# Turning an operand through memory: four quadrant stores and one load, in place of one store and four loads

## The chip, the cores and the metric

The kernel runs on one core of one Trainium2 chip. The metric is device time in microseconds (us) of one execution. Five engines have a queue each: TensorE (PE, with its weight loads shown as PEld), VectorE (DVE), ScalarE (ACT), GpSimd (POOL) and SyncE (SP), which here only issues DMAs. Every DMA of this kernel stands in SP's queue, and SP works it off in order: when the DMA at its head has to wait, all that stand behind it wait too.

## The reference

Two layers, each of a linear attention block and a mixture-of-experts block (PEER, one expert per head), on 2048 rows of 576 numbers in float32:

```python
x = A_x
x = x + _A_ref(_layernorm(x, axis=-1), A_wqkv, A_wo)
x = x + _B_ref(_layernorm(x, axis=-1), B_w_q, B_k1, B_k2, B_u, B_v)
x = x + _A_ref(_layernorm(x, axis=-1), A_wqkv, A_wo)
x = x + _B_ref(_layernorm(x, axis=-1), B_w_q, B_k1, B_k2, B_u, B_v)
```

`_A_ref` multiplies by `wqkv`, takes a positive map `phi` of q and k, sums `k^T v` over all rows for 32 heads of 18, divides `q (k^T v)` by `q sum(k)`, and multiplies by `wo`. `_B_ref` scores 8 + 8 keys per head, takes the best of each, looks up one row of `u` and one of `v` (64 experts), and adds `gelu(x . u) v` over the heads.

## The kernel before

The 2048 rows are 16 tiles of 128 rows (partitions); `l` is the layer, `t` the tile. The front of a layer makes q, k and v of each tile and sums the state of the attention (`front_T`, `front_k`, `front_v`, `front_q`, `front_state`). The back of a layer divides, multiplies by `wo`, adds the residual and normalizes (`back_scale`, `back_oT`, `back_out`), scores and selects the experts (`exp_y`, `exp_scores`, `exp_select`, `exp_gelu`) and adds their output (`exp_out`). A layer's back and the next layer's front overlap: in the stretch from 290 to 480 us each step works on three tiles, the o of tile t, the b of tile t-1 and the f of layer 1 of tile t-3.

A matmul needs its operand with the contracted dimension on the partitions, so each tile is transposed three times per layer: `f` (input of q, k, v), `o` (attention output, ahead of `wo`) and `b` (input of the scores). `turned` chooses one of two ways by the table `SQUARES`. In `transposed`, TensorE does five transposes of 128 x 128. In `squares`, TensorE does nothing: VectorE transposes all 32 x 32 squares of the tile (line 229), and what is left, the exchange of whole squares between partition quadrants, goes through memory in `moved`: a store of r to a tile `y_d` in memory, and loads of it into g. Then ScalarE rounds g to the high part thi, and VectorE subtracts to get the low part tlo (`split`, lines 117 and 118). 42 turns go this way: 23 of f (twelve of layer 0, eleven of layer 1), 10 of o (layer 0, tiles 6 to 15) and 9 of b (layer 0, tiles 5 to 13). In the profile their tiles are rf, y_df, gf, thif, tlof, and the same with o and b.

The order of TensorE, ScalarE, VectorE and GpSimd is written out by hand (the strings given to `play`) and pinned by `in_order`. SP is not pinned: a scheduler places the DMAs in SP's queue by when it reckons them due. The DMAs share eight semaphores in rotation; an SP row waits for the DMA eight places ahead of it, if nothing earlier in the queue has waited for that already. `g` lies in one of two buffers taken in turn (tags uhi and ulo), and r and the normalized y share three buffers (tag y), so a buffer is written again only when the store that reads it has landed.

Other DMAs that stand beside the turns in SP's queue: `pq` (the stored phi(q) of a tile, line 441), `x` (residual input, 436), `x_d` (its result, 617), `hl_d` (the turned f kept for a later pass, 333 and 334), `fold` (weights of layer 0's front, 631).

## Time and profile before

| what | us |
|---|---|
| median of 3 runs | 719.97 |
| lowest and highest run | 719.19, 720.18 |
| the profiled execution, its time | 720.89 |
| its span in the profile | 719.1 |
| busy: TensorE / VectorE / ScalarE / GpSimd | 698.8 / 474.0 / 320.9 / 202.7 |

The granted clock of TensorE is 0.997 over the span. DMA engines are busy 46.7% of the span on average, 0.76 in the stretch 340.7 to 350.8. A row of a timeline reads: start in us, length in us, engine, line, operation, tile written <- tiles read, count, and in brackets the idle time of the engine ahead of it with what ended that. SPq rows are issues: their length is the time SP takes to hand the DMA over, and the transfer lands later.

### The profile page before, as it was taken

How to read it: one execution, taken by the hardware profiler on the slowest of the kernel's cores; microseconds unless marked ns; L12 is line 12 of the kernel's file. 1: busy time of each engine (PE TensorE's matmuls, PEld its weight loads, DVE VectorE, ACT ScalarE, POOL GpSimd, SP SyncE). 2: the span in 40 equal slices, each digit the busy share in tenths (PEclk: the TensorE clock that was granted, in tenths of full speed). 3: DMA queues.
4: the chain of work that ended last, by engine and by line, in shares of the span. 5: the costliest groups of instructions: out<-in, count | busy, mean ns of one | idle time of the engine just before them, and what ended most of it. 6: DMA issues, size and time to landing. Idle time of an engine off the chain costs nothing. (4 is left out here: it accounts for less than half of the span.)

```text
span 719.1 us, 14715 instructions
## 1 busy us (share of the span) xinstructions
PE 698.8 (97%) x5464; PEld 649.9 (90%) x5464; DVE 474.0 (66%) x1031; ACT 320.9 (45%) x658; POOL 202.7 (28%) x543
## 2 busy tenths in 40 slices
PE   8999999999999999999999999999999999999995
PEld 6999989999998999899898989899899999899984
DVE  5533343435437877687787878552647798988996
ACT  4522422342224456455555554644543534444443
POOL 2211000111004533344343433210323244433431
PEclk9999999999999999999999999999999999999998
DMA  8847777774312322476767665423632324111101
GB/s 252 274 159 249 262 237 260 253 216 137 112 33 67 100 103 102 147 232 199 238 219 234 205 198 172 138 61 121 170 106 83 112 71 134 51 67 51 51 17 66
DMA packets 82711, 107.17 MB, mean 149 GB/s; under 512 B 8976, under 2 KB 47376, under 8 KB 82640
## 3 DMA queue, kind: packets, MB, share of 16 engines
q1 hardware_dynamic: 82640, 106.24, 46.7%
q8 instruction: 43, 0.70, 0.4%
q14 instruction: 28, 0.23, 0.1%
HBM read 68.88 MB, written 37.32 MB: 148 GB/s over the span
## 5 line engine op out<-in xcount | busy, mean ns | idle before, releaser
L483 PE MATMUL ppo<-ohi,thio 126*128 126x252 f32 (+1 forms) x320 | 50.6, 300 | 3.9 <-ACT thio L117 3.9
L483 PEld LDWEIGHTS ppo<-ohi,thio 126*128 126x128 f32 (+1 forms) x320 | 44.9, 189 | 5.8 <-ACT thio L117 4.9
L188 ACT ACTIVATE junk<-x,mb 128x576 bf16<-128x576 f32 x32 | 24.8, 775 | 49.0 <-POOL mb L187 43.0
L205 ACT ACTIVATE yb<-x,rsb 128x640 f32<-128x640 f32 x32 | 29.5, 921 | 35.7 <-POOL rsb L195 35.7
L258 PE MATMUL ppk<-whi,thif 128*128 128x252 f32 (+1 forms) x300 | 45.2, 297 | 0.1
L258 PE MATMUL ppv<-whi,thif 128*128 128x252 f32 (+1 forms) x300 | 44.7, 295 | 0.1
L179 POOL TENSOR_SCALAR rsf<-mvf 128x1 f32<-128x1 f32 x16 | 3.4, 211 | 146.9 <-DVE mvf L176 146.8
L453 POOL TENSOR_TENSOR o<-pq,zb 128x576 f32<-128x576 f32 x19 | 27.3, 1439 | 60.9 <-ACT zb L399 57.4
L258 PE MATMUL ppv<-whi,tlof 128*128 128x252 f32 (+1 forms) x300 | 43.9, 293 | 0.0
L258 PE MATMUL ppk<-whi,tlof 128*128 128x252 f32 (+1 forms) x300 | 43.9, 293 | 0.0
L258 PEld LDWEIGHTS ppk<-whi,thif 128*128 128x128 f32 x300 | 40.9, 188 | 3.1 <-issue 2.9
L258 PEld LDWEIGHTS ppv<-whi,thif 128*128 128x128 f32 x300 | 41.3, 188 | 1.1 <-issue 0.4
L258 PEld LDWEIGHTS ppk<-whi,tlof 128*128 128x128 f32 x300 | 41.2, 188 | 0.0
L258 PEld LDWEIGHTS ppv<-whi,tlof 128*128 128x128 f32 x300 | 41.2, 188 | 0.0
L483 PE MATMUL ppo<-olo,thio 126*128 126x252 f32 (+1 forms) x256 | 39.6, 293 | 0.0
L258 PE MATMUL ppq<-whi 128*128 128x252 f32 (+1 forms) x260 | 39.5, 299 | 0.0
L483 PE MATMUL ppo<-ohi,tloo 126*128 126x252 f32 (+1 forms) x256 | 39.5, 293 | 0.0
L277 DVE TENSOR_SCALAR ek<-ek 128x576 f32<-128x576 f32 x16 | 7.4, 460 | 46.2 <-ACT ek L276 46.2
L258 PEld LDWEIGHTS ppq<-whi 128*128 128x128 f32 x260 | 36.0, 189 | 0.6 <-DVE eq L287 0.3
L483 PEld LDWEIGHTS ppo<-olo,thio 126*128 126x128 f32 x256 | 36.2, 188 | 0.0
L258 PE MATMUL ppk<-wlo,thif 128*128 128x252 f32 x240 | 36.1, 293 | 0.0
L258 PE MATMUL ppv<-wlo,thif 128*128 128x252 f32 x240 | 36.1, 293 | 0.0
(205 smaller groups left out, 1781.5 us busy)
## 6 DMA issues: line engine op xcount, KB each, us to landing
fold<-in_wq_t SPq DMA_DIRECT2D x64, 288.0 KB, 4.2
whi<-hl_d SPq DMA_DIRECT2D x26, 320.0 KB, 4.4
y_df<-rf SPq DMA_DIRECT2D x23, 320.0 KB, 3.0
gf<-y_df SPq DMA_DIRECT2D x92, 80.0 KB, 2.1
pq_d<-eq SPq DMA_DIRECT2D x19, 288.0 KB, 2.2
pq<-pq_d SPq DMA_DIRECT2D x19, 288.0 KB
xf<-in_x SPq DMA_DIRECT2D x16, 288.0 KB, 2.7
x<-in_x SPq DMA_DIRECT2D x16, 288.0 KB, 2.7
```

What stands on the lines that cost most here:

```text
L179: nc.gpsimd.tensor_scalar(rs[:, 0:1], mv[:, 1:2], EPS_LN, 1.0, op0=ALU.add, op1=ALU.mult)
L188: nc.scalar.activation(junk, xt, AF.Square, bias=m[:, 0:1], accum_out=m[:, 1:2])
L205: nc.scalar.activation(y, x2, AF.Identity, scale=rs[:, 0:1], bias=rs[:, 1:2])
L258: nc.tensor.matmul(o[:, at:at + c1 - c0], tt[a == "lo"][:, b, :], wb[:, cols + c0:cols + c1], start=(i == 0), stop=(i == len(todo) - 1))
L277: nc.vector.tensor_scalar(e, e, 1.0, EPS, op0=ALU.min, op1=ALU.add)
L453: nc.gpsimd.tensor_tensor(o[:, :D], pq, zb, op=ALU.mult)
L483: nc.tensor.matmul(p[:, at:at + c1 - c0], hl[a][:r, b], w[:r, c0:c1], start=(i == 0), stop=(i == len(todo) - 1))
```

## The change

`moved` lays the tile in memory out differently. Before, a row of `y_d` is a row of r, written by one store of all 128 partitions; each of four loads then fills one partition quadrant of g from pieces of 160 numbers (640 bytes) of all rows. After, a row of `y_d` is a row of g: four stores, one for each partition quadrant of r, write pieces of 640 bytes to all rows, and one load brings all 128 partitions of g as whole rows of 2560 bytes. What g holds is the same, and so are the bytes moved and the number of DMAs (five).

```diff
-        d = dr.tile([P, NB * P], F32, name=f"y_d{n}")
-        nc.sync.dma_start(d, r)
+        d = dr.tile([P, 4, NB * 32], F32, name=f"y_d{n}")
+        for q in range(4):
+            nc.sync.dma_start(d.rearrange("(j i) q x -> q i j x", j=4)[q], r[32 * q:32 * q + 32].rearrange("i (j x) -> i j x", j=4))
         yield
...
-        for j in range(4):
-            nc.sync.dma_start(g[32 * j:32 * j + 32], d.rearrange("(q i) (j x) -> j i q x", q=4, j=4)[j])
+        nc.sync.dma_start(g, d)
         return g
```

The order of instructions on TensorE, VectorE, ScalarE and GpSimd is the same before and after. SP's is not, since the scheduler places the new DMAs. In the names below the numbers are layer and tile (y_do0_9 is the o of layer 0, tile 9), the last number a buffer's.

SP's queue around the o turn of tile 9 (from about 340.7 us), before:

```order
L231 DMA y_do0_9_4473<-ro0_9_4471 128x640
L333 DMA hl_d5_93<-thif1_5_4469 128x640
L334 DMA hl_d5_93<-tlof1_5_4470 128x640
L237 DMA go0_9_4607<-y_do0_9_4473 32x4x160
L617 DMA x_d6_142<-x20_6_4489 128x576
L237 DMA go0_9_4607<-y_do0_9_4473 32x4x160
L231 DMA y_db0_8_4595<-rb0_8_4593 128x640
L237 DMA go0_9_4607<-y_do0_9_4473 32x4x160 x2
L231 DMA y_df1_6_4620<-rf1_6_4618 128x640
L237 DMA gb0_8_4622<-y_db0_8_4595 32x4x160 x4
L237 DMA gf1_6_4644<-y_df1_6_4620 32x4x160 x4
L231 DMA y_do0_10_4665<-ro0_10_4663 128x640
```

The same place of SP's queue after:

```order
L232 DMA y_do0_9_4473<-ro0_9_4471 32x4x160 x4
L617 DMA x_d6_142<-x20_6_4492 128x576
L333 DMA hl_d5_93<-thif1_5_4469 128x640
L334 DMA hl_d5_93<-tlof1_5_4470 128x640
L232 DMA y_db0_8_4598<-rb0_8_4596 32x4x160 x4
L237 DMA go0_9_4613<-y_do0_9_4473 128x640
L232 DMA y_df1_6_4623<-rf1_6_4621 32x4x160 x4
L237 DMA gb0_8_4628<-y_db0_8_4598 128x640
L441 DMA pq0_12_4894<-pq_d0_12_116 128x576
L237 DMA gf1_6_4647<-y_df1_6_4623 128x640
L232 DMA y_do0_10_4665<-ro0_10_4663 32x4x160 x4
```

All of go now stands behind all of y_db, where half of it stood ahead, and the load of pq for tile 12 has moved from behind y_do of tile 10 to the place ahead of gf. The o turns of tiles 7, 11 and 13 look alike, except that tile 13 is the last of them.

SP's queue at that last one (from about 411 us), before:

```order
L231 DMA y_db0_12_5579<-rb0_12_5577 128x640
L237 DMA go0_13_5591<-y_do0_13_5457 32x4x160 x2
L231 DMA y_df1_10_5604<-rf1_10_5602 128x640
L237 DMA gb0_12_5606<-y_db0_12_5579 32x4x160 x4
L237 DMA gf1_10_5628<-y_df1_10_5604 32x4x160 x4
L231 DMA y_do0_14_5649<-ro0_14_5647 128x640
```

and after:

```order
L232 DMA y_db0_12_5582<-rb0_12_5580 32x4x160 x4
L237 DMA go0_13_5597<-y_do0_13_5457 128x640
L232 DMA y_df1_10_5607<-rf1_10_5605 32x4x160 x4
L237 DMA gb0_12_5612<-y_db0_12_5582 128x640
L232 DMA y_do0_14_5649<-ro0_14_5647 32x4x160
L237 DMA gf1_10_5631<-y_df1_10_5607 128x640
L232 DMA y_do0_14_5649<-ro0_14_5647 32x4x160 x3
```

Here the first piece of the store y_do of tile 14 stands ahead of the load gf.

SP's queue at the first o turn (tile 6, from about 293.4 us), before:

```order
L231 DMA y_do0_6_3737<-ro0_6_3735 128x640
L231 DMA y_db0_5_3778<-rb0_5_3776 128x640
L237 DMA go0_6_3759<-y_do0_6_3737 32x4x160 x4
L617 DMA x_d3_139<-x20_3_3782 128x576
L237 DMA gb0_5_3804<-y_db0_5_3778 32x4x160 x4
L231 DMA y_df1_3_3891<-rf1_3_3889 128x640
```

and after:

```order
L232 DMA y_do0_6_3737<-ro0_6_3735 32x4x160 x4
L232 DMA y_db0_5_3778<-rb0_5_3776 32x4x160 x2
L237 DMA go0_6_3762<-y_do0_6_3737 128x640
L232 DMA y_db0_5_3778<-rb0_5_3776 32x4x160 x2
L617 DMA x_d3_139<-x20_3_3785 128x576
L232 DMA y_df1_3_3891<-rf1_3_3889 32x4x160
L237 DMA gb0_5_3807<-y_db0_5_3778 128x640
```

Half of y_db now stands behind go, and the load gb behind the first piece of the store y_df.

## The prediction

> **What bounds the kernel now.** First the page's busy times, then the list of what TensorE waits for, then the timeline of each place in that list.

> ```profile
> PE 698.8 (97%) x5464; PEld 649.9 (90%) x5464; DVE 474.0 (66%) x1031; ACT 320.9 (45%) x658; POOL 202.7 (28%) x543
> ```

> ```profile
> PE ppo L483 <- ACT thio L117: 3.9, 4, 1.4
> ```

> TensorE is busy for 698.8 of 719.1 us, and its instructions stand in the same order before and after the change. So the change can move the end only through the time TensorE waits. The first view gives the ceiling: 20.3 us of idle time in the whole run. The second says what part of it hangs on a turned operand: four waits of 3.9 us together, all of the output product (ppo) for the rounded operand thio, which ScalarE makes from the tile go. No other row of that list names a tile that passes through memory. The timeline shows where they are, and two starts that have little room:

> ```profile
> 302.58 1.59 PE L483 MATMUL ppo<-ohi,thio 126*128 126x252 f32 x10 [1.40 <-ACT thio L117]
> 318.89 1.56 PE L483 MATMUL ppo<-ohi,thio 126*128 126x252 f32 x10
> 351.57 1.59 PE L483 MATMUL ppo<-ohi,thio 126*128 126x252 f32 x10 [0.83 <-ACT thio L117]
> 384.33 1.59 PE L483 MATMUL ppo<-ohi,thio 126*128 126x252 f32 x10 [0.89 <-ACT thio L117]
> 417.05 1.59 PE L483 MATMUL ppo<-ohi,thio 126*128 126x252 f32 x10 [0.83 <-ACT thio L117]
> ```

> These are the o turns of tiles 6, 7, 9, 11 and 13. ScalarE's rows say what it waited for there:

> ```profile
> 301.80 0.73 ACT L117 ACTIVATE thio<-go 128x640 fp32r<-128x640 f32 x1
> ...
> 317.88 0.74 ACT L117 ACTIVATE thio<-go 128x640 fp32r<-128x640 f32 x1 [1.01 <-DMA go<-y_do]
> ...
> 350.78 0.74 ACT L117 ACTIVATE thio<-go 128x640 fp32r<-128x640 f32 x1 [2.38 <-DMA go<-y_do]
> ...
> 383.55 0.74 ACT L117 ACTIVATE thio<-go 128x640 fp32r<-128x640 f32 x1 [2.44 <-DMA go<-y_do]
> ...
> 416.26 0.74 ACT L117 ACTIVATE thio<-go 128x640 fp32r<-128x640 f32 x1 [2.38 <-DMA go<-y_do]
> ```

> For tile 6 the row has no idle time ahead of it (no bracket): ScalarE comes to thio from other work, so the 1.40 us there is not the memory's. For the odd tiles it sits idle until go lands, and TensorE waits behind it (for tile 7 it starts 0.27 us after thio is done at 318.62). So the landing of go in the odd tiles of this stage decides.

> **What the odd tiles' queue does.** SP's rows for tile 9, and the y_db store of the three others:

> ```profile
> 344.24 0.32 SPq L237 DMA_DIRECT2D go<-y_do  x1
> ...
> 345.69 0.34 SPq L231 DMA_DIRECT2D y_db<-rb  x1
> 346.08 2.00 SPq L237 DMA_DIRECT2D go<-y_do  x2
> ...
> 352.40 1.73 SPq L237 DMA_DIRECT2D gf<-y_df  x4
> ...
> 355.19 0.55 SPq L441 DMA_DIRECT2D pq<-pq_d  x1
> ```

> ```profile
> 314.16 0.61 SPq L231 DMA_DIRECT2D y_db<-rb  x1
> ...
> 378.56 0.41 SPq L231 DMA_DIRECT2D y_db<-rb  x1
> ...
> 411.17 0.37 SPq L231 DMA_DIRECT2D y_db<-rb  x1
> ```

> Two loads of go are issued early (344.24 is the first, when the store y_do has landed), but the last two of the four stand behind the store y_db of the next turn, which waits for VectorE's transpose of rb. From the issue of y_db to the start of thio it takes 3.72, 5.09, 4.99 and 5.09 us (317.88 - 314.16, 350.78 - 345.69, 383.55 - 378.56, 416.26 - 411.17). The order after the change puts all four pieces of y_db, and then the one load of go, at this place. The gate (rb) stays; what follows it changes.

> **The change, priced.** Per turn one store of 320 KB and four loads of 80 KB become four stores of 80 KB and one load of 320 KB: five issues either way, 210 for the 42 turns, the same bytes. Four issues in a row take 1.73 us (the gf row), 0.43 each, so a fifth starts some 1.8 us after the first. A landing is priced from these rows (KB each, median us from issue to landing):

> ```profile
> y_df<-rf SPq DMA_DIRECT2D x23, 320.0 KB, 3.0
> ...
> x<-in_x SPq DMA_DIRECT2D x16, 288.0 KB, 2.7
> ...
> x<-x_d SPq DMA_DIRECT2D x16, 288.0 KB, 3.3
> ...
> go<-y_do SPq DMA_DIRECT2D x40, 80.0 KB, 3.9
> ```

> No 320 KB load in one piece stands in the trace in this stage. 2.7 (a load of an input) is the low end, 3.9 (go itself, in the crowd of this stage) the high end. I take 3.3, since that load reads back what a store wrote, in one piece, as the new one does.

> Odd tiles, go. From the issue of y_db to thio: 1.8 + 3.3 + 0.1 = 5.2 us. Against the four numbers above this is +1.48, +0.11, +0.21 and +0.11; tile 7 has 0.27 of room, so +1.2. Sum +1.6 us. With 2.7 it is +0.6 - 0.5 - 0.4 - 0.5 = -0.8; with 3.9 it is +1.8 + 0.7 + 0.8 + 0.7 = +4.0.

> [...] The trace has both: 2.7 for 288 KB of an input, 3.3 for the same bytes written shortly before; no run here shows which the new load is like.

> Last odd tile (13), gf. For the last f of this pattern the new order puts the load of gf behind the first piece of the y_do of tile 14, which waits for VectorE's ro:

> ```profile
> 420.24 0.34 SPq L231 DMA_DIRECT2D y_do<-ro  x1
> ```

> ```profile
> 421.28 0.74 ACT L117 ACTIVATE thif<-gf 128x640 fp32r<-128x640 f32 x1 [1.98 <-DMA gf<-y_df]
> 422.61 0.78 ACT L188 ACTIVATE junk<-x,mb 128x576 bf16<-128x576 f32 x1 [0.59 <-POOL mb L187]
> ...
> 431.50 0.73 ACT L117 ACTIVATE thio<-go 128x640 fp32r<-128x640 f32 x1
> ```

> ```profile
> 432.86 1.50 PE L483 MATMUL ppo<-ohi,thio 126*128 126x252 f32 x10
> ```

> gf goes out at 420.24 + 0.4 = 420.64. The queue is empty but for one 80 KB store, so 2.7 us: thif starts at 423.4 and ends at 424.2 instead of 422.0. The squares behind it (junk) start at 424.2 instead of 422.61, 1.6 us later, and the layernorms that hang on them carry that to thio: 433.1, done at 433.8, where TensorE wants it at 432.86. So +1.0 us; +1.6 with 3.3; 0 if the chain in between has slack that I take for dependent work.

> Other odd tiles, gf. There the new order puts the load of pq ahead of gf, and pq waits for VectorE to finish reading its buffer:

> ```profile
> 352.67 0.82 DVE L461 TENSOR_TENSOR o<-pq,r 128x576 f32<-128x576 f32 x1
> ```

> ```profile
> 355.96 0.74 ACT L117 ACTIVATE thif<-gf 128x640 fp32r<-128x640 f32 x1 [1.31 <-DMA gf<-y_df]
> 357.13 0.78 ACT L188 ACTIVATE junk<-x,mb 128x576 bf16<-128x576 f32 x1 [0.43 <-POOL mb L187]
> ...
> 366.02 0.73 ACT L117 ACTIVATE thio<-go 128x640 fp32r<-128x640 f32 x1
> ```

> ```profile
> 367.38 1.50 PE L483 MATMUL ppo<-ohi,thio 126*128 126x252 f32 x10
> ```

> pq goes out at 353.5, gf at 353.9, and lands at 356.6 (2.7) to 357.2 (3.3): thif is 0.7 to 1.3 us late. junk had 0.43 of idle time ahead of it, so 0.3 to 0.9 goes on to thio, which has 0.63 of room (366.75 to 367.38). I take 0. That cover is the thinnest: beyond a landing of 3.3, three tiles lose up to 0.6 each, 1.8 us in all.

> First pair, gb of tile 5. In the new order the load of gb waits behind the first piece of y_df, for VectorE's rf:

> ```profile
> 302.40 0.34 SPq L231 DMA_DIRECT2D y_df<-rf  x1
> ```

> ```profile
> 306.39 1.40 PE L525 MATMUL kva<-shi,thib 128*128 128x512 f32 x5
> ```

> It goes out at 302.8 and lands at 305.5, thib is done at 306.3, and TensorE wants it at 306.39: 0 us, with 0.6 at a landing of 3.3. For tile 6 itself thio is held by ScalarE's own work, 0.

> The twelve f turns of layer 0, ahead of 200 us, have loads that lie long before their use:

> ```profile
> 95.20 1.75 SPq L237 DMA_DIRECT2D gf<-y_df  x4
> ```

> ```profile
> 104.26 0.73 ACT L117 ACTIVATE thif<-gf 128x640 fp32r<-128x640 f32 x1
> ```

> Loads issued until 96.95 are used at 104.26: several us of room, 0. VectorE and ScalarE wait for one DMA instead of four ahead of each split, and for four instead of one before they write a buffer that a store still reads: 0, both beside TensorE's work. No queue but SP's changes its order.

> Sum: +1.6 + 1.0 = +2.6 us. The profiled execution took 720.89 us with a span of 719.1, so it becomes 723.5 and 721.7. The median of the runs shown, 719.97, is 0.9 below the profiled one, and becomes 722.6.

> **Rivals.** *No change.* Landings go by 2.7: -0.8 + 1.0 = +0.2, 720.2 us. For it: the input loads. [...] Against it: four stores of 80 KB, just ahead of the load in the same queue, must drain first.

> *Faster.* The load of go lands as early as 2.1 to 2.2 us after its issue, because nothing is in its way once y_do, x_d and hl_d have gone out earlier. Then tiles 9, 11 and 13 lose nearly all their 0.83, 0.89 and 0.83 us, tile 7 costs nothing, and if gf of tile 13 is also covered the time is 719.97 - 2.5 = 717.5. It decides from a landing of about 2.4 us downward. Against it: no single load of this size in the rows is so quick.

> *Much slower.* Writing pieces of 640 bytes to memory may cost more than reading them. The rows that bound it, whole y_db rows written and then g loads alone in flight (DMA share and GB/s at the end):

> ```profile
> 297.75:298.25 0.50, 0.50 (x6) 0.50 (x5) 0.43 (x3) 0.38 (x1) 0.09 (x1) 1.00 0.98 379
> ...
> 96.60:98.00 1.40, 1.40 (x13) 1.40 (x12) 1.30 (x3) 0.00 (x0) 0.00 (x0) 1.00 0.79 224
> ```

> Rows of 2560 bytes are written at 379 GB/s; pieces of 640 are read at 224. I took 224 for writing them too, which the spacing of the issues hides. At half of it, 320 KB take 2.9 us instead of 1.5, go is 1.4 later in four tiles and the cover of the other odd tiles is gone: +5.6 + 1.8 on the forecast, 730 us.

> **Chances and range.** "Same" is within 0.2% (1.44 us), about what a measurement of this kernel can tell from no change. My forecast (721.4 to 725) 0.50, much slower 0.10, no change 0.27, faster 0.13. So slower 0.60, same 0.27, faster 0.13. The range takes the low ends (-0.8 and 0: 719.2) and the high ends (4.0 + 1.6 + 1.8 + 0.6 = 8.0: 728.0).

> **What would show it.** Right: TensorE's waits for thio longer than 0.9 us in tiles 11 and 13 and a new one of about 1 us in tile 7; a gap before the ppo that now starts at 432.86; thif of tile 10 near 423.4 in TensorE's unshifted time; one load of go landing 3.3 us after its issue. Wrong: waits for thio that shrink, a load that lands within 2.7 us, or stores of 80 KB whose landing passes 4 us, which would pull gb and gf after them.

## The result, and the profile after

The changed kernel takes 729.64 us (median of 4 runs, 728.96 to 730.56), the kernel before beside it 720.08 us (4 runs). The ratio is 1.0130, 95% interval 1.0116 to 1.0144: 9.4 us slower, where 2.6 us were forecast and 728.0 was the upper end of the range. The profiled execution has a span of 728.0 us against 719.1.

The busy times and TensorE's wait for thio, from the page and the list of waits:

```profile
PE 702.9 (97%) x5464; PEld 652.8 (90%) x5464; DVE 474.6 (65%) x1031; ACT 320.9 (44%) x658; POOL 202.6 (28%) x543
```

```profile
PE ppo L483 <- ACT thio L117: 7.3, 6, 1.8
```

The waits for thio have grown from 3.9 to 7.3 us. That is 3.4 of the 8.9 us in the span. TensorE's busy time has also grown, by 4.1 us, with the same instructions. TensorE's timeline at the o turns (tiles 6, 7, 9, 10, 11, 13 and 14) shows where:

```profile
303.40 1.59 PE L483 MATMUL ppo<-ohi,thio 126*128 126x252 f32 x10 [1.40 <-ACT thio L117]
...
321.70 1.59 PE L483 MATMUL ppo<-ohi,thio 126*128 126x252 f32 x10 [0.95 <-ACT thio L117]
...
355.15 1.58 PE L483 MATMUL ppo<-ohi,thio 126*128 126x252 f32 x10 [1.30 <-ACT thio L117]
...
371.30 1.59 PE L483 MATMUL ppo<-ohi,thio 126*128 126x252 f32 x10 [0.19 <-ACT thio L117]
...
389.07 1.82 PE L483 MATMUL ppo<-ohi,thio 126*128 126x252 f32 x10 [1.62 <-ACT thio L117]
...
424.49 2.79 PE L483 MATMUL ppo<-ohi,thio 126*128 126x252 f32 x10 [1.80 <-ACT thio L117]
...
441.83 1.50 PE L483 MATMUL ppo<-ohi,thio 126*128 126x252 f32 x10
```

Against the same rows of the kernel before (302.58, 318.89, 351.57, 367.38, 384.33, 417.05, 432.86) TensorE's lag is 0.82, 2.81, 3.58, 3.92, 4.74, 7.44 and 8.97 us. So 0.8 us is lost before the o turns begin, and then more with every pair of tiles. After tile 14 the lag stays. From tile 11 to tile 13 it grows by 2.70, though the wait at 13 is only 0.97 longer than before (1.80 - 0.83). From 13 to 14 it grows by 1.53 without any wait. In both places the ten matmuls take longer (1.82 and 2.79 us instead of 1.59). A table by stretches says why. Each row has the stretch and its length, the busy time of TensorE, its weight loads, VectorE, ScalarE and GpSimd with their counts, the granted clock, the DMA share and GB/s:

```profile
386.86:390.26 3.40, 1.78 (x22) 1.54 (x19) 1.34 (x4) 1.98 (x4) 0.17 (x1) 1.00 0.79 242
390.26:393.67 3.41, 3.41 (x16) 3.41 (x16) 2.22 (x3) 1.11 (x2) 0.43 (x3) 0.50 0.46 132
393.67:397.08 3.41, 3.41 (x19) 2.91 (x18) 2.33 (x4) 1.61 (x4) 0.70 (x1) 1.00 0.48 152
420.98:424.39 3.41, 1.61 (x26) 1.15 (x24) 1.15 (x4) 0.69 (x2) 0.20 (x1) 1.00 0.74 198
424.39:427.80 3.41, 3.31 (x14) 3.31 (x15) 2.90 (x5) 2.43 (x5) 0.60 (x3) 0.50 0.28 93
```

Behind each of the two longest waits TensorE runs at half clock for 3.41 us, which delays it by up to 1.7 us each (half of 3.41). Nothing in the kernel before's profile showed this: there the granted clock is at 0.50 only from 714.7 us to the end at 719.1.

The turns' other loads are late too. ScalarE's and SP's rows around tile 11:

```profile
388.28 0.74 ACT L117 ACTIVATE thio<-go 128x640 fp32r<-128x640 f32 x1 [3.14 <-DMA go<-y_do]
...
395.41 0.74 ACT L117 ACTIVATE thif<-gf 128x640 fp32r<-128x640 f32 x1 [4.04 <-DMA gf<-y_df]
```

```profile
382.44 2.55 SPq L232 DMA_DIRECT2D y_db<-rb  x4
385.03 0.43 SPq L237 DMA_DIRECT2D go<-y_do  x1
385.56 1.91 SPq L232 DMA_DIRECT2D y_df<-rf  x4
387.58 0.37 SPq L237 DMA_DIRECT2D gb<-y_db  x1
391.07 0.34 SPq L441 DMA_DIRECT2D pq<-pq_d  x1
391.62 0.32 SPq L237 DMA_DIRECT2D gf<-y_df  x1
```

Here, in tile 11, the four y_db issues take 2.55 us instead of the 1.8 I had assumed. In tiles 7, 9 and 13 they do take 1.8, but there the one issue of go takes 0.45, 0.93 and 1.21 us. In tile 11 the load of go takes from 385.03 to 388.28. gf goes out only behind pq, 4.1 us after the last store of y_df, and ScalarE idles 4.04 us for it. The new loads' landing, from the list of DMA issues:

```profile
gf<-y_df SPq DMA_DIRECT2D x23, 320.0 KB, 4.2
...
go<-y_do SPq DMA_DIRECT2D x10, 320.0 KB, 3.6
...
gb<-y_db SPq DMA_DIRECT2D x9, 320.0 KB, 3.0
```

### The profile page after: what moved, and what is told of

The parts are those of the page before. It is cut to its first block, busy times and chain, and to the rows that moved or that the text cites. A ratio compares the mean times of both kernels' runs of the same rounds, so it can differ in the third digit from the quotient of the medians.

```text
span 728.0 us, 14652 instructions
## 1 busy us (share of the span) xinstructions
PE 702.9 (97%) x5464; PEld 652.8 (90%) x5464; DVE 474.6 (65%) x1031; ACT 320.9 (44%) x658; POOL 202.6 (28%) x543
## 5 line engine op out<-in xcount | busy, mean ns | idle before, releaser
L483 PE MATMUL ppo<-ohi,thio 126*128 126x252 f32 (+1 forms) x320 | 52.2, 307 | 7.3 <-ACT thio L117 7.3
L483 PEld LDWEIGHTS ppo<-ohi,thio 126*128 126x128 f32 (+1 forms) x320 | 45.9, 193 | 9.8 <-ACT thio L117 8.9
L188 ACT ACTIVATE junk<-x,mb 128x576 bf16<-128x576 f32 x32 | 24.8, 774 | 46.9 <-POOL mb L187 40.9
L483 PE MATMUL ppo<-olo,thio 126*128 126x252 f32 (+1 forms) x256 | 40.8, 300 | 0.0
L483 PE MATMUL ppo<-ohi,tloo 126*128 126x252 f32 (+1 forms) x256 | 40.0, 295 | 0.0
L483 PEld LDWEIGHTS ppo<-olo,thio 126*128 126x128 f32 x256 | 37.6, 195 | 0.0
L118 DVE TENSOR_TENSOR tlof<-gf,thif 128x640 fp32r<-128x640 f32 x23 | 18.9, 822 | 27.4 <-ACT thif L117 27.3
L483 PEld LDWEIGHTS ppo<-ohi,tloo 126*128 126x128 f32 x256 | 36.7, 191 | 0.0
## 6 DMA issues: line engine op xcount, KB each, us to landing
fold<-in_wq_t SPq DMA_DIRECT2D x64, 288.0 KB, 4.2
pq_d<-eq SPq DMA_DIRECT2D x19, 288.0 KB, 2.1
pq<-pq_d SPq DMA_DIRECT2D x19, 288.0 KB
xf<-in_x SPq DMA_DIRECT2D x16, 288.0 KB, 2.7
x<-in_x SPq DMA_DIRECT2D x16, 288.0 KB, 2.9
```

Source lines behind the costliest of these rows:

```text
L118: eng.tensor_tensor(lo, src, hi.bitcast(F32), op=ALU.subtract)
L188: nc.scalar.activation(junk, xt, AF.Square, bias=m[:, 0:1], accum_out=m[:, 1:2])
L483: nc.tensor.matmul(p[:, at:at + c1 - c0], hl[a][:r, b], w[:r, c0:c1], start=(i == 0), stop=(i == len(todo) - 1))
```

## The experiments

Three theories were open at the start. A: what costs is the place in SP's queue, since go, gb and gf stand behind more issues. B: writing in pieces of 640 bytes is slow. C: four stores and one load are slower as such, turn by turn. Two came later: D, which is A with the four stores of y_db as what the rest is built on, and E, transfers of instructions that meet those stores. Each ratio below is to the kernel before run beside it, with its 95% interval.

**Go ahead of the y_db stores, in the changed kernel.** In the string that sets the order of the loop, the o turn's load moves ahead of the b turn's transpose:

```diff
-... v1.-2 st1.-3 bT0.1 sel0.0 gel0.0 oT0.2 v1.-2 num0.3 ...
+... v1.-2 st1.-3 oT0.2 bT0.1 sel0.0 gel0.0 v1.-2 num0.3 ...
```

> The new form, with one piece of the written-out order moved: in the odd tiles the load of go is asked for ahead of the transpose of rb, so in SP's queue it stands ahead of the four y_db stores instead of behind them. Theory A (place in the queue): the 5.7 us that TensorE waits for thio in tiles 7, 9, 11 and 13 (0.95, 1.30, 1.62, 1.80) go, and with them the two stretches of half clock (3.1 us): 729.6 - 8.8 = 720.8 us, between 719 and 723. In exchange gf of the odd tiles stands behind the first piece of the next y_do; tile 13 has that already and pays nothing. Theory B (writing in pieces of 640 bytes is slow, wherever the load stands): go, gb and gf land late as before, no more than the wait behind y_db itself is saved, and the time stays above 726 us.

Measured: 725.74 us, ratio 1.0054 (1.0033 to 1.0074). The waits for thio in tiles 7, 11 and 13 are gone, tile 9 keeps 0.72, and no half clock comes (1.00 from 388 to 395 and from 422 to 429 us). But the time falls by little more than half of what was expected, since the next operands are late in their turn: the products of tiles 8 and 10 now wait 0.44 and 0.42 us for thio, and the scores of tile 11 wait for thib. TensorE's rows of tile 11:

```profile
387.20 1.59 PE L483 MATMUL ppo<-ohi,thio 126*128 126x252 f32 x10
...
392.34 1.43 PE L525 MATMUL kva<-shi,thib 128*128 128x512 f32 x5 [1.20 <-ACT thib L117]
```

So the place of go is one part, and gb behind the stores is another.

**Whole rows in place of pieces.**

```diff
-            nc.sync.dma_start(d.rearrange("(j i) q x -> q i j x", j=4)[q], r[32 * q:32 * q + 32].rearrange("i (j x) -> i j x", j=4))
+            nc.sync.dma_start(d.rearrange("p q x -> p (q x)")[32 * q:32 * q + 32], r[32 * q:32 * q + 32])
```

> The new form with the same number, size and order of DMAs, but each of the four stores writes 32 whole rows of 2560 bytes in place of 128 pieces of 640 bytes. The exchange of squares between the partition quadrants is thereby left out, so the operands are other numbers; no instruction's size changes. Theory A (place in the queue): the same waits for thio in tiles 7, 9, 11 and 13 (each within 0.3 us), half clock at the same two places, 729.6 us within 1.5. Theory B (the pieces): stores land at least 0.5 us sooner, the four waits shrink by 0.5 us or more each, the half clock goes with them, 721 to 725 us.

Measured: 731.25 us, ratio 1.0133 (1.0108 to 1.0157), the same as the whole change; TensorE's waits for thio, in the list of waits:

```profile
PE ppo L483 <- ACT thio L117: 7.3, 7, 1.6
```

Theory B falls: in this kernel the size of the pieces costs nothing that shows (1.0133 against 1.0130). Two parts of theory A's expectation failed. The wait of tile 13 is 1.15 us instead of 1.80, and the two stretches of half clock did not come in the profiled execution of this kernel (1.00 from 388 to 395 and from 422 to 429 us). Its span is 727.0 us all the same.

**Filling the idle time.** Eight matmuls of constants ahead of the output product of tiles 11 and 13, in the changed kernel:

```diff
-        todo = sorted(out_passes(), key=lambda x: x[1]) if t == 0 else out_passes()
+        todo = sorted(out_passes(), key=lambda x: x[1]) if t == 0 else out_passes(); [nc.tensor.matmul(p[:, :252], ohi[:126, 0, :P], ohi[:126, 0, :252], start=True, stop=True) for _ in range(8 if l == 0 and t in (11, 13) else 0)]
```

> The new form, with eight extra matmuls of constants ahead of the output product of tiles 11 and 13. They lie in the time in which TensorE waits for thio there, take about 1.2 us of the 1.6 and 1.8, and are overwritten by the product. Theory A (the long idle time itself halves the clock afterwards): TensorE idles less than 0.7 us at once in these two places, the granted clock stays 1.00 there, and 3.1 us go: 726.5 us. Rival (the halved clock has another cause, or belongs to that run alone): the two stretches at half clock stay, or others come, and the time is 729.6 us within 0.7.

Measured: 729.98 us, ratio 1.0115 (1.0094 to 1.0136). That is some 1 us below the whole change's 1.0130, and the intervals overlap. TensorE's row and the stretch behind it:

```profile
387.50 1.18 PE L480 MATMUL ppo<-ohi 126*128 126x252 f32 x8
389.68 1.59 PE L483 MATMUL ppo<-ohi,thio 126*128 126x252 f32 x10 [1.01 <-ACT thio L117]
```

```profile
390.26:393.67 3.41, 3.41 (x27) 3.39 (x26) 2.81 (x6) 1.76 (x3) 0.60 (x3) 1.00 0.35 93
```

The clock stays at 1.00, as theory A says, but the 3.1 us do not come back. At full clock TensorE is earlier at the next operand and waits for it longer: in tile 11 it is held for 1.18 + 1.01 us, in tile 13 for 1.17 + 1.48. So here the half clock went with the long waits (0.50 behind them in the changed kernel, 1.00 in the same place with the time filled), and most of what that costs, perhaps all, would be waited anyway.

**Go ahead of the y_db store, in the kernel before.** The same move of one word as above.

> The kernel before, with the same move: all four loads of go stand ahead of the y_db store in the odd tiles, where two of them stood behind it. Theory A (place in the queue): TensorE's waits for thio in tiles 9, 11 and 13 (0.83, 0.89, 0.83 us) go, 720.0 - 2.5 = 717.5 us. Rival (the loads land late because the engines are crowded there, and not because they are issued late): the waits stay within 0.3 us and the time is 720 us within 0.7.

Measured: 721.59 us, ratio 0.9999 (0.9986 to 1.0012). The waits for thio shrink to 0, 0.26 and 0 us in tiles 9, 11 and 13, but the gain is given back. VectorE's transpose of rb, SP's rows and TensorE's for tile 11:

```profile
377.98 0.85 DVE L229 STREAM_TRANSPOSE rb<-yb 128x640 f32<-128x640 f32 x1 [0.65 <-DMA y_do<-ro]
```

```profile
379.76 1.58 SPq L237 DMA_DIRECT2D go<-y_do  x1
381.38 0.43 SPq L231 DMA_DIRECT2D y_db<-rb  x1
```

```profile
388.44 1.43 PE L525 MATMUL kva<-shi,thib 128*128 128x512 f32 x5 [0.42 <-ACT thib L117]
```

rb is ready at 378.83 and its store goes out at 381.38, behind the loads of go. The scores of tiles 9, 11 and 13 now wait 0.29, 0.42 and 1.44 us for thib, where they waited for nothing before. Part of the delay in tile 11 is not the order's: the last issue of go takes 1.58 us there, where 0.43 is usual (see the last experiment).

**One kind or two at a time.** The name n begins with the kind. The edit is shown for o alone, against the changed kernel; for the others the letter is "b" or "f", and for pairs `n[0] in "ob"`, "of" and "fb":

```diff
-        d = dr.tile([P, 4, NB * 32], F32, name=f"y_d{n}")
-        for q in range(4):
-            nc.sync.dma_start(d.rearrange("(j i) q x -> q i j x", j=4)[q], r[32 * q:32 * q + 32].rearrange("i (j x) -> i j x", j=4))
+        d, new = dr.tile([P, 4, NB * 32], F32, name=f"y_d{n}"), n[0] == "o"
+        for q in range(4 if new else 1):
+            nc.sync.dma_start(d.rearrange("(j i) q x -> q i j x", j=4)[q] if new else d.rearrange("p q x -> p (q x)"), r[32 * q:32 * q + 32].rearrange("i (j x) -> i j x", j=4) if new else r)
...
-        nc.sync.dma_start(g, d)
+        [nc.sync.dma_start(g[32 * j:32 * j + 32], d.rearrange("(q i) j x -> j i q x", q=4)[j]) for j in range(0 if new else 4)]; new and nc.sync.dma_start(g, d)
```

> Only the ten o turns go the new way; f and b stay as before. In SP's queue the odd tiles then have one store of y_db and right behind it the one load of go. Theory A (what costs is what stands between the transpose of rb and the landing of go): 0.35 us for the store and 3.3 for the load in place of 5.0 from the issue of y_db to thio, so the waits for thio in tiles 9, 11 and 13 (0.83, 0.89, 0.83 us) go, and no half clock comes: 2.5 us less than the kernel before, a ratio of 0.9965. Theory C (four quadrant stores and one load are slower as such, whatever stands beside them): go lands later, the waits for thio grow, and the ratio is 1.003 or more.

> Only the nine b turns go the new way. Four stores of y_db then stand ahead of the last two loads of go in the odd tiles. Theory A: go there is asked for 1.4 us later and lands 1.4 us later, in four tiles, so 5.3 us more than before, with half clock (1.5 us each) where the wait passes some 1.6 us: a ratio of 1.007 to 1.012, the largest of the three kinds. Theory C: cost in proportion to the turns, 9 of 42 of the whole 9.5 us, so 2 us, 1.003.

> Only the 23 f turns go the new way. The load of gf stays ahead of pq in the queue here. Theory A: gf of layer 0's tile 8 is late as in the whole change (+0.7); in the odd tiles the four stores of y_df stand ahead of gb, 1.4 us later, of which some 0.5 is covered at the scores of three tiles: +0.7 + 2.7, a ratio of 1.003 to 1.006, and no half clock. Theory C: 23 of 42 of 9.5 us, 5.2 us, 1.007, spread over both layers' turns.

> The o and b turns go the new way, f stays as before. The odd tiles have the whole change's order up to go (four stores of y_db, then go), but one store of y_df, and gf is not behind pq. Theory A: the waits for thio of the odd tiles that the whole change has at first (about +1.2, +0.5, +0.7, +1.0) remain or are a little smaller, since each turn's delay is no longer added to by gf; what goes is +0.7 at layer 0's tile 8, the small waits at tiles 8, 10, 12 and 14 (0.3 to 0.7 each) and most of the half clock: a ratio of 1.003 to 1.006. Rival (f has no part in it): 1.012 or more.

> o and f go the new way, b stays as before, with the reference's numbers this time: the whole change with only the b turns taken back. Theory D (the four stores of y_db, ahead of go and of gb, are what the rest is built on): as with one store for b, ratio 0.998 to 1.001, though o and f, 33 of the 42 turns, go the new way. Rival (taking back a kind gives back its own +3.0 us): 1.009.

> f and b go the new way, o stays as before. Alone they cost 1.7 and 3.0 us. If the costs add up: +4.7 us, ratio 1.0066. Theory D (four stores of y_db followed by four of y_df make gf go out behind pq and everything behind them late, whatever o does): 1.009 to 1.013, the most of any two kinds, with waits for thio of 1.2 us and more in tiles 9, 11 and 13.

Measured, with the kernel before and the whole change:

| new form for | ratio | 95% interval |
|---|---|---|
| none | 1 | |
| o (10 turns) | 0.9991 | 0.9981 to 1.0001 |
| f (23) | 1.0024 | 1.0011 to 1.0036 |
| b (9) | 1.0042 | 1.0027 to 1.0058 |
| o and f (33) | 1.0015 | 0.9991 to 1.0039 |
| o and b (19) | 1.0070 | 1.0057 to 1.0084 |
| f and b (32) | 1.0159 | 1.0128 to 1.0190 |
| all (42) | 1.0130 | 1.0116 to 1.0144 |

Theory C falls: 33 turns of o and f cost about nothing (2.8 us at the end of the interval), 9 turns of b cost 3.0 us. The costs do not add up. Alone the three make +4.1 us, together +9.4; b costs 3.0 us alone, 5.7 on top of o, 9.7 on top of f. The pair f and b is worse than all three. Its SP rows and TensorE's in an even tile:

```profile
403.09 2.77 SPq L232 DMA_DIRECT2D y_db<-rb  x4
...
408.67 0.30 SPq L232 DMA_DIRECT2D y_df<-rf  x1
409.15 0.34 SPq L237 DMA_DIRECT2D gb<-y_db  x1
```

```profile
413.09 1.43 PE L525 MATMUL kva<-shi,thib 128*128 128x512 f32 x5 [0.19 <-ACT thib L117]
417.56 1.58 PE L258 MATMUL ppv<-whi,thif 128*128 128x252 f32 x10 [0.41 <-ACT thif L117]
```

There the load gb stands behind the first piece of the next store y_df, which waits for VectorE's rf, so TensorE now waits in the even tiles too. Theory D expected 1.009 to 1.013 for this pair; 1.0159 came, with an interval from 1.0128. Theory A has the places right and the sizes wrong. For only_b it expected 1.007 to 1.012, and 1.0042 came, which is nearer to the 1.003 of theory C; for ob_new 1.003 to 1.006, and 1.0070 came. For only_o it expected 0.9965, and 0.9991 came: from the issue of go to thio it takes 3.6 to 4.6 us in tiles 7, 9 and 11 instead of the 3.3 assumed, and the products there still wait 0.46, 0.51 and 0.79 us.

**One store for b.** In the whole change, y_db alone goes out in one DMA of whole rows. For b this leaves out the exchange between the quadrants.

```diff
-        d = dr.tile([P, 4, NB * 32], F32, name=f"y_d{n}")
-        for q in range(4):
-            nc.sync.dma_start(d.rearrange("(j i) q x -> q i j x", j=4)[q], r[32 * q:32 * q + 32].rearrange("i (j x) -> i j x", j=4))
+        d, m = dr.tile([P, 4, NB * 32], F32, name=f"y_d{n}"), 1 if n[0] == "b" else 4
+        for q in range(m):
+            nc.sync.dma_start(d.rearrange("(j i) q x -> q i j x", j=4)[q] if m > 1 else d.rearrange("p q x -> p (q x)"), r[32 * q:32 * q + 32].rearrange("i (j x) -> i j x", j=4) if m > 1 else r)
```

> The new form for all three kinds, but y_db is stored by one DMA of whole rows in place of four of 640-byte pieces; the exchange of squares between quadrants is left out for b, so the scores are other numbers. In the odd tiles go then stands behind one store instead of four. Theory A (the four issues of y_db ahead of go): go lands 1.4 us earlier, the waits of 0.95 to 1.80 us shrink by 0.9 to 1.4 each, no half clock: 5 to 7 us less than the whole change, ratio 1.003 to 1.006. Rival (the landing of the one load of go, whatever stands ahead of it): waits within 0.4 us of the whole change's, ratio 1.010 or more.

Measured: 721.93 us, ratio 0.9993 (0.9979 to 1.0007): all of the 9.4 us are gone. SP's and TensorE's rows of tile 11:

```profile
381.05 0.32 SPq L232 DMA_DIRECT2D y_db<-rb  x1
381.54 0.32 SPq L237 DMA_DIRECT2D go<-y_do  x1
```

```profile
386.90 1.58 PE L483 MATMUL ppo<-ohi,thio 126*128 126x252 f32 x10 [0.88 <-ACT thio L117]
```

With of_new this shows that the four stores of y_db are what the whole loss is built on. It is more than theory A had expected (1.003 to 1.006); its price per wait leaves out gb and gf behind the same stores, which is a reason that no run here tests.

**Go ahead, only o new.** The edit for o alone, and with it

```diff
-... v1.-2 st1.-3 bT0.1 sel0.0 gel0.0 oT0.2 v1.-2 num0.3 ...
+... v1.-2 st1.-3 oT0.2 bT0.1 sel0.0 gel0.0 v1.-2 num0.3 ...
```

> Only the o turns go the new way, and the load of go stands ahead of the y_db store. With the old form of o this place in the queue held y_db up, since four loads of go take 2.6 to 3.4 us to hand over; the new form hands over one. Theory A (SP's queue decides): the waits for thio in tiles 7, 9, 11 and 13 go (0.65, 0.70, 0.98 and 0 where the load stood behind y_db), rb's store starts within 0.3 us of its transpose, and no new wait for thib above 0.3 us comes: 2.5 to 3.5 us less than the kernel before, ratio 0.995 to 0.9965. Rival (the engines that move the data are the limit, not the queue): go lands as late or gb later, ratio 0.999 or more.

Measured: 721.17 us, ratio 0.9987 (0.9973 to 1.0000), about 1 us, within what can be told from no change. The 0.995 to 0.9965 that theory A expected did not come. The waits for thio in the odd tiles are gone; TensorE waits 0.23 and 1.53 us for thib in tiles 9 and 11 instead.

**Two DMAs per turn.** One store and one load of whole rows for all kinds. The edit is against the kernel with one store for b.

```diff
-        d, m = dr.tile([P, 4, NB * 32], F32, name=f"y_d{n}"), 1 if n[0] == "b" else 4
+        d, m = dr.tile([P, 4, NB * 32], F32, name=f"y_d{n}"), 1
```

> One store of whole rows and one load of whole rows per turn, two DMAs in place of five; the exchange between quadrants is left out. In the queue go then stands ahead of y_db in the odd tiles, and gf of each odd tile ahead of pq. Theory A (what costs is the time that SP takes to hand over the DMAs of a turn one after the other): faster than both kernels, by the waits of the kernel before for thio (2.5 us) and up to 1 us of others, ratio 0.995 to 0.9975. Theory C (a load of 320 KB in one piece lands later than four of 80 KB, and that is what costs): ratio 1.002 or more, with waits for gb and gf.

Measured: 717.17 us, ratio 0.9933 (0.9906 to 0.9959). The waits for thio are down to tile 6's 1.4 us:

```profile
PE ppo L483 <- ACT thio L117: 1.4, 1, 1.4
```

The same bytes in two issues instead of five are 4.8 us faster than the kernel before. That is more than the 0.995 to 0.9975 expected. This kernel leaves the exchange out, so it shows what fewer issues would be worth and is no version to use. A load of 320 KB in one piece is not the trouble here.

**What halves the clock.** In the kernel before, at the output products of layer 1's tiles 2 to 10:

```diff
+        k = {2: 2, 3: 4, 4: 5, 5: 6, 6: 7, 7: 8, 8: 9, 9: 11, 10: 13}.get(t, 0) if l else 0
+        if k:
+            s = wk.tile([P, P], F32R, tag="probe", name=f"probe{n}", bufs=1)
+            nc.tensor.matmul(p[:, :252], ohi[:126, 0, :P], ohi[:126, 0, :252], start=True, stop=True)
+            for _ in range(k):
+                nc.vector.tensor_copy(s, p[:, :P])
+            nc.tensor.matmul(p[:, :252], s[:126], ohi[:126, 0, :252], start=True, stop=True)
```

> The kernel before, with a wait of chosen length put into TensorE's stream at nine output products of layer 1 (tiles 2 to 10), where no turn goes through memory: a matmul of constants, 2 to 13 copies of 128x128 of its result by VectorE one after the other, and a matmul that needs the last copy. It asks what idle time of TensorE halves its clock. Theory A (idle time inside one stretch of 3.41 us on a fixed grid decides, from about 1.6 us): the short waits leave the clock at 1.00; those that put more than 1.6 us of idle time into one stretch are followed by 3.41 us at 0.5, which add up to 1.7 us each to the time beside the waits. Rival (it takes a whole idle stretch, 3.4 us or more, and the half clock seen had another cause): the clock stays at 1.00 at all nine.

Measured: 771.87 us, ratio 1.0686; the nine waits add up to 35.9 us, longer than meant, as VectorE comes to the copies late. TensorE's rows of two waits, and stretches of some 3.4 us around the second of them and around one of the long ones:

```profile
593.08 0.38 PE L487 MATMUL ppo<-ohi,probe 126*128 126x252 f32 x1 [1.81 <-DVE probe L486]
599.76 0.38 PE L487 MATMUL ppo<-ohi,probe 126*128 126x252 f32 x1 [2.01 <-DVE probe L486]
```

```profile
595.63:599.04 3.41, 2.12 (x17) 1.88 (x15) 2.17 (x6) 0.00 (x0) 0.00 (x0) 1.00 0.23 87
599.04:602.45 3.41, 2.69 (x20) 2.69 (x21) 3.27 (x12) 0.09 (x1) 0.19 (x1) 1.00 0.51 173
...
677.50:681.00 3.50, 0.71 (x7) 0.51 (x5) 2.89 (x7) 2.61 (x5) 0.85 (x4) 0.99 0.00 0
681.00:684.40 3.40, 0.00 (x0) 0.00 (x0) 3.06 (x12) 0.92 (x1) 2.37 (x5) 0.50 0.00 0
```

The waits of 1.81 and 2.01 us leave the clock at 1.00: around the first the two stretches (588.80 to 592.20 and 592.20 to 595.60) hold 0.93 and 0.88 us of idle time, around the second 1.29 and 0.72. A stretch idle for 2.79 of 3.50 us is followed by 0.50. So in these runs it was not the length of one wait that went with the half clock (a wait of 1.62 us did in the changed kernel, one of 2.01 did not here), and a stretch did not have to be idle as a whole.

**Do transfers of instructions cost it?** The DMA records of the kernel before and of the changed kernel hold 43 transfers of 16 KB each on the instruction queue, one every 16.7 us on average in the first and every 17.7 us in the second between 285 and 445 us. In that stretch the two profiles have 367 DMA issues. Of the 23 that overlap such a transfer 13 take over 0.65 us, of the 344 others 2. In the changed kernel six of the nine transfers there met the y_db stores or the load of go behind them. More small matmuls at the start move them against the rest:

```diff
+            c = (16, 16) if i < n - 8 and n > 2 else (P, 512)
-            nc.tensor.matmul(p[:, :512], junk[:, :P], junk[:, :512], start=True, stop=True)
+            nc.tensor.matmul(p[:c[0], :c[1]], junk[:, :c[0]], junk[:, :c[1]], start=True, stop=True)
...
-        warm_up(14)
+        warm_up(78)
```

With 78 it is half a period (after_half, before_half), with 46 a quarter and with 142 a whole one.

> The new form, with 64 more matmuls (16 columns, of constants) among those that warm TensorE up at the start, 128 instructions more. The traces hold a transfer of 16 KB on the instruction queue some every 17 us, 43 in all, one for each 254 of TensorE's 10,928 instructions; in ten profiles 47 of the 52 DMA issues of over 0.65 us between 285 and 445 us overlap one. In the whole change it meets the stores of y_db or the load of go behind them in seven tiles; 128 instructions move it half a period, some 8.5 us. Theory E (this coincidence makes the four y_db stores dear): y_db's four issues take 1.8 us in all tiles and go's 0.4, and TensorE's lag behind the kernel before grows between 306 and 441 us by 4 to 5.5 us in place of 7.9. Theory D (the place in the queue alone): by 7.5 to 8.5 us as before. The start costs both the same 1 to 3 us.

> The new form with 32 more matmuls at the start, 64 instructions, which moves the transfers of instructions a quarter of their period, some 4.3 us earlier. They then meet the issues that stand 4 us ahead of y_db: x_d, hl_d, or nothing. Theory E: as with half a period, the lag grows by 4 to 6 us between 306 and 441 us. Theory D: by 7.5 to 8.5 us.

> The new form with 128 more matmuls at the start, 256 instructions, a whole period: the transfers of instructions meet the same DMA issues as in the whole change. Both theories: the lag grows by 7 to 8.5 us between 306 and 441 us; it shows what the longer start alone costs, 2 to 5 us, all of it ahead of 20 us.

> The kernel before with the same 64 matmuls at the start. Both theories: the start costs as much as in the new form, 1 to 3 us; behind it the lag behind the kernel before stays within 1 us between 306 and 441 us, since its one store of y_db leaves little for such a transfer to meet.

Measured: after_half 1.0140 (1.0112 to 1.0169), after_quarter 1.0141 (1.0096 to 1.0185), after_full 1.0138 (1.0101 to 1.0175), before_half 0.9980 (0.9965 to 0.9996). The move worked. Tile 11 of after_half:

```profile
383.95 1.78 SPq L232 DMA_DIRECT2D y_db<-rb  x4
385.77 0.45 SPq L237 DMA_DIRECT2D go<-y_do  x1
```

```profile
389.97 1.58 PE L483 MATMUL ppo<-ohi,thio 126*128 126x252 f32 x10 [1.01 <-ACT thio L117]
```

The four issues take 1.78 us and go 0.45, and the time of the whole kernel is the same. From the scores of tile 5 (306.39 in the kernel before) to the product of tile 14 (432.86) TensorE's lag grows from 1.1 to 9.0 us in the whole change, and from 1.7 to 10.3, 1.3 to 9.8 and 0.8 to 9.3 in after_half, after_quarter and after_full: 7.9, 8.6, 8.6 and 8.5 us. In after_half the waits for thio in tiles 9, 11 and 13 do shrink, to 0.89, 1.01 and 1.40 us, but TensorE waits for other operands instead, 1.14 us of it for thib at the scores of tile 5. As the cause of the total theory E falls, and the place in the queue remains. That the transfers cost as much at whatever issues they meet instead is not excluded. The longer start cost nothing that the total shows, where 1 to 5 us had been expected. The kernel before became 1.4 us faster by the shift (0.3 to 2.5), which neither theory had expected; the cause of that stays open.

## Why the prediction was wrong

The sign and the main place were right: slower, through TensorE's waits for thio in tiles 7, 9, 11 and 13, because go stands behind four stores of y_db. The time was not: +9.4 us instead of +2.6, 1.6 us above the range. TensorE's lag says where it was lost, with two more starts of the product, tile 8 (337.70, before 334.67) and tile 12 (406.46, before 400.15), and the row just ahead of tile 7's (320.43, before 318.79):

| where | lag added, us | forecast, us |
|---|---|---|
| ahead of the o turns (0.6 of it at layer 0's tile 8) | 0.8 | 0 |
| first pair, up to tile 7 | 0.8 | 0 |
| go, tiles 7, 9, 11 and 13 | 3.7 | 1.6 |
| tiles 8 and 10, behind gf | 0.6 | 0 |
| half clock, behind the waits of tiles 11 and 13 | 3.1 | 0 |
| gf of the last odd tile, at tile 14 | none seen | 1.0 |
| sum | 9.0 | 2.6 |

The steps that failed are above all the term of go, which came to 3.7 us for 1.6, and the clock, which the sum does not have. A wait adds 0.1 to 0.2 us more to the lag than its own length, since TensorE's rows otherwise overlap (in the kernel before the row ahead of 367.38 ends at 367.55). By the steps:

- *Odd tiles, go: +1.6.* Mis-sized. From the issue of y_db to thio I had 1.8 + 3.3 + 0.1 = 5.2 us; it is 5.21, 5.53, 5.84 and 6.07 in tiles 7, 9, 11 and 13 (388.28 - 382.44 in tile 11). In tile 11 the four issues took 2.55 us instead of 1.8, in tiles 9 and 13 go's own issue took 0.93 and 1.21. The waits grew by 0.95, 0.47, 0.73 and 0.97 us (0.83, 0.89, 0.83 in the kernel before), 3.1 in all, inside the step's own upper end of 4.0.
- *TensorE's clock.* No step had it. Behind two waits of over 1.6 us (1.62 and 1.80) the clock was 0.50 for 3.41 us each, some 3 us of the lag in the profile. By keep_clock it is not an independent 3 us: without it TensorE waits longer at the next operands, and the kernel was only some 1 us faster.
- *Other odd tiles, gf: 0.* Here the landing was mis-sized, and the cover nearly held. gf went out behind pq as foreseen, but ScalarE waited 3.3, 3.6 and 4.0 us for it in tiles 7, 9 and 11 instead of the 2.0 to 2.6 that the forecast makes (1.31 + 0.7 to 1.3). In the rows of tile 11, thif starts 6.8 us later than before (395.41 against 388.58), where go's product starts 4.7 later. By ScalarE's order this delays the squares, the normalized y and thio of the next tile, but the products of tiles 8, 10 and 12 wait for thio only 0.03, 0.19 and 0 us. It goes no further: the rb ahead of go in tiles 9, 11 and 13 starts 3.14, 4.03 and 6.45 us later than before, hardly more than TensorE's lag by then (3.03, 3.92 and 6.31). No run here changed the place of gf alone, and why f and b are dear together stays open.
- *Last odd tile, gf of layer-1 tile 10: +1.0.* gf was late as described, but the product of tile 14 shows no wait: the half clock had already delayed TensorE by more. In keep_clock, at full clock, TensorE does wait for thio there (0.43 us in its row).
- *First pair, gb: 0.* Some 0.2 us: the lag is 0.82 at tile 6 (303.40 - 302.58) and 1.06 at the scores of tile 5 (307.45 - 306.39), with one more wait of 0.28 us for thif behind it; by the row ahead of tile 7's product it is 1.64.
- *The twelve f turns of layer 0: 0.* Failed at one, for some 0.6 us. I read several us of room from one turn (95.20 to 104.26) for all twelve. At tile 8 the load now stands behind the stores of the next turn. SP's rows, and TensorE's wait:

```profile
165.52 4.21 SPq L232 DMA_DIRECT2D y_df<-rf  x8
169.90 0.34 SPq L237 DMA_DIRECT2D gf<-y_df  x1
```

```profile
173.77 1.42 PE L258 MATMUL ppk<-whi,thif 128*128 128x252 f32 x9 [0.62 <-ACT thif L117]
```

- *The sum.* The places do add up, as the table shows; their sizes were wrong. By keep_clock, though, a right price for the clock alone would have been too much, as most of it would be waited at the next operands. And a price for one kind of turn would not have served: b's 9 turns cost 3.0 or 9.7 us, by what f does.
- *Rivals.* "Much slower", 730 us with a chance of 0.10, has the right time by luck and the wrong mechanism: whole rows change nothing. "Faster" asked for a landing of go below 2.4 us; it was 3.6. "No change" rested on 2.7.

What stays open is what each of go behind y_db, gb behind y_df and gf behind pq would cost without the others, since moving one of them shifts the wait to the next.

## What to carry to other kernels

Here four issues in place of one, in a queue that is worked off in order, put what stands behind them 1.4 us later (1.8 against 0.4); before splitting a store, list what stands behind it in the queue and who waits for that. When several operands pass through the same queue in a loop, don't add up the prices of single kinds: here they make 4.1 us alone and 9.4 together, so undo the change by kinds and in pairs. A move in the queue that removes one wait has not gained anything until the next operand's wait has been looked at.

## What the runs showed of the hardware

```profile
384.89:388.30 3.41, 1.87 (x14) 1.70 (x14) 1.69 (x3) 2.42 (x4) 0.29 (x1) 1.00 0.65 213
388.30:391.72 3.42, 3.42 (x23) 3.19 (x23) 2.87 (x6) 1.41 (x2) 0.63 (x3) 1.00 0.73 202
```

Long DMA issues on SP went with the transfers of instructions here: 13 of the 15 of over 0.65 us counted above overlap one, and in after_half, which shifts the transfers, the issues of tile 11 that took 2.55 us (y_db) took 1.78. The shift changed nothing in the changed kernel's total (1.0140 against 1.0130) and made the kernel before 1.4 us faster (0.3 to 2.5).
